# Two-layer decode attention: both wq at the head of the stream, PV in pieces, and another order of the last slabs

## The chip, the core and the metric

The kernel runs on one NeuronCore of a Trainium2 chip. The core has TensorE (PE, matrix products into PSUM), VectorE (DVE), ScalarE (ACT), GpSimd (POOL), and SyncE (SP), whose queue here only issues DMAs. Sixteen DMA engines move data between HBM and the on-chip memory. The metric is the device time of one execution in microseconds; the time of a kernel is the median of its runs.

## The reference

Two independent problems, A and B, have the same shapes. Each decodes one token for a batch of 2, with 32 query heads on 16 key/value heads of width 128, over the last 4096 positions of a cache:

```python
q = (x @ wq).reshape(B, Sq, Hq, Dh).transpose(0, 2, 1, 3)    # x: 2 x 1 x 576, wq: 576 x 4096
...
k = jnp.repeat(k_cache[:, :, Sk - W:, :], rep, axis=1) # W = 4096, rep = 2
v = jnp.repeat(v_cache[:, :, Sk - W:, :], rep, axis=1)
scores = jnp.einsum("bhqd,bhkd->bhqk", q, k) * (Dh ** -0.5)
p = _softmax(scores, axis=-1)
o = jnp.einsum("bhqk,bhkd->bhqd", p, v)
return o.transpose(0, 2, 1, 3).reshape(B, Sq, Hq * Dh) @ wo        # wo: 4096 x 576
```

The two results are concatenated along the last axis. All inputs and outputs are bf16.

## The kernel before

**Slabs.** The heads are worked in 16 steps s, eight for A and eight for B (`ND = 16`). A step takes four (batch, head) pairs: their keys are one slab K of 128 x 16384 bf16 (4096 KB), their values another slab V. Slabs land in `ring`, which has four slots (`NR = 4`).

**The stream.** A list `stream` fixes the order in which SP issues the large loads. The item number n goes into slot n % 4, and its DMA waits for the last reader of item n - 4 (`deps = [reader[n - NR]]`). SP is in order: a DMA that waits holds up every DMA behind it. The list begins Q0 (A's wq), K0, K1, V0, K2, V1, Q1 (B's wq), K3, V2, K4, V3, ..., because Q1 is put in at step `WQ_AT = 3`. wq has 576 rows; 512 go into a ring slot and the last 64 into the small tile `wqr`, by a second DMA. The output weights `wo` are loaded per group of two steps, just ahead of one of the K slabs. The last V slab (V15) is loaded as five pieces (64, 32, 16, 8 and 8 of 128 column blocks), each with its own semaphore.

**One step.** (a) `do_X` (L407): eight DVE transposes bring K to the form that PE needs. (b) `do_S` (L428, L431): PE forms the scores in two PSUM banks. (c) `do_max` (L440) takes maxima per row; `do_nm` turns them on PE (`Tm`, L446), reduces them (L453) and scales them (L458); `do_exp` spreads the result (L463, L470), takes exp on ACT (L475) and transposes the weights p to `pC` (L481). (d) `do_sum` turns the row sums on PE (L487), adds them (L494), takes the reciprocal (L499) and spreads it (L500, L506). (e) `do_PV` (L522): 32 matmuls of p with V into the bank `ACC`, for the step before, s - 1; ACT then evicts `ACC` (L534). (f) For step s - 2, `do_comb` (L555) gathers the evicted sums into `OT`, `do_norm` (L571) normalises on DVE, and once per two steps `do_redist` and `do_proj` (L592, L622) multiply with `wo`. Of the last two steps each is projected by itself. In the last V slab, the final two pieces go through `do_PVb` (L543), which writes `OT` directly.

**The q projection.** `do_qproj(G)` (L359, L367, L373, L381) makes q for two steps: ten matmuls into two of the banks `tb`, two evictions on ACT, one transpose and four copies on DVE. Four groups serve A and run before step 0. The four of B run inside step 3, one after every second transpose of K. The last reader of a wq slot is the last matmul of its fourth group.

**Order.** Each engine runs its operations in the order of the program text, and operations wait for each other by semaphores; nothing is reordered later. On PE, an operation that waits holds up all behind it. The four banks `st` hold two steps' scores; the two banks `tb` are taken in turn by all small jobs.

Of the kernel before, what the change touches and what calls it, by code (L numbers as in the profile page):

```python
# [6 lines left out]
BF16 = mybir.dt.bfloat16  # L7
# [52 lines left out]
def build_kernel(nc, probs, out, cfg=None):  # L60
    cfg = dict(cfg or {})
    NR = cfg.get("NR", 4)
    NKT = cfg.get("NKT", 5)
    NPT = cfg.get("NPT", 3)
    LS = 1
    NZQ = 2
    WQ_AT = cfg.get("WQ_AT", 3)

    x0, k0, v0, wq0, wo0 = probs[0]
    NPROB = len(probs)  # L70
    Bb, _one, D = x0.shape
    _, Hkv, Sk, Dh = k0.shape
    HD = wq0.shape[1]
# [7 lines left out]
    JR = 16  # L81
    NRD = NJ // JR
    SPP = Hkv // 2
    ND = SPP * NPROB
    NG = ND // 2
    GPP = SPP // 2
    NFC = D // 128
    DREM = D - 128 * NFC
    assert DREM * 2 == 128 and NFC * HD == SLABW
    HH = HD // 2  # L90
# [8 lines left out]
    PIECES = [(0, 64), (64, 96), (96, 112), (112, 120), (120, 128)]  # L99
    NPC = len(PIECES)  # L100
# [5 lines left out]
    with es:  # L106
        block = es.enter_context(nc.Block())
        sb = lambda name, shape, dt: es.enter_context(nc.sbuf_tensor(name, shape, dt))
        ring = sb("ring", [128, NR, SLABW], BF16)
        xt = sb("xt", [128, NKT, 1024], FP32)  # L110
        wqr = sb("wqr", [128, HH], BF16)
        wob = sb("wob", [128, 2, 8, NOUT], BF16)
        xT = sb("xT", [128, NPROB, NXC, 128], BF16)
        x_dup = sb("x_dup", [Bb, NPROB, 2, DREM, 2], BF16)
# [40 lines left out]
        wq_sem = [sem("wq%d" % r) for r in range(NPROB)]  # L155
# [42 lines left out]
            return last  # L198
        x_cd = S.add("dve", f_xd, [x_zd, x_dma], "xdup")

        stream = []
        for s_ in range(ND + LS):
            if s_ == 0 or s_ == WQ_AT:
                stream.append(("Q", 0 if s_ == 0 else 1))
            if s_ < ND:
                stream.append(("K", s_))
            if s_ >= LS:
                stream.append(("V", s_ - LS))
        pos = {key: n for n, key in enumerate(stream)}
        w_at = {}  # L210
        for G in range(NG):
            s_ = 2 * G + 2 if by_group(G) else 2 * G + 1
# [3 lines left out]
        pieces = []  # L216
# [3 lines left out]
        qproj = {}  # L220
# [3 lines left out]
        def issue_slab(n):  # L224
            kind, D_ = stream[n]
            if kind == "Q":
# [16 lines left out]
        def issue_wq(n, P):  # L243
            wqP = probs[P][3]
            r = n % NR
            deps = [reader[n - NR]] if n >= NR else []
            slab_dma[n] = dma_op("sp", ring_sem[r], 1, lambda e: e.dma_start(
                ring[:, r, :], wqP[0:NFC * 128, :].rearrange("(p s) n -> p (s n)", s=NFC)).then_inc(ring_sem[r], 16), deps, "wq%d" % P)
            deps = [qproj[(P * GPP - 1, 1)]] if P >= 1 else []
            wq_dma[P] = dma_op("sp", wq_sem[P], 1, lambda e: e.dma_start(  # L250
                wqr[:, :], wqP[NFC * 128:D, :].rearrange("r (h n) -> r h n", h=2)).then_inc(wq_sem[P], 16), deps, "wqr%d" % P)

        def issue_wo(G):
            woP = probs[G // GPP][4]
# [90 lines left out]
        def do_qproj(G):  # L345
            P = G // GPP
            nq = pos[("Q", P)]
            issue_until(nq)
            evs = []
            for nb in range(2):  # L350
                hf = nb
                c0 = nb * HH + 512 * (G % GPP)

                def fn(e, bank, c0=c0, hf=hf):
                    last = None
                    for ch in range(NFC + 1):
                        w_ = ring[:, nq % NR, ch * HD + c0:ch * HD + c0 + 512] if ch < NFC else wqr[:, c0 - hf * HH:c0 - hf * HH + 512]
                        x_ = xT[:, P, ch if ch < NFC else NFC + hf, :]
                        last = e.matmul(bank[:, 0:512], x_, w_, start=(ch == 0), stop=(ch == NFC))  # L359
                    return last  # L360
                n, bank, op = tb_job(fn, "q%d_%d" % (G, nb), [slab_dma[nq], wq_dma[P], op_xev])
                qproj[(G, nb)] = op
                reader[nq] = op
                d = [op]
                if G >= 1:
                    d.append(chain[(G - 1, "qtr")])
                evs.append(S.add("act", lambda e, bank=bank, nb=nb: e.activation(qrow[:, 512 * nb:512 * nb + 512], bank[:, 0:512], ACTF.Copy),  # L367
                                 d, "qrow%d_%d" % (G, nb)))
                tb_consumer[n] = evs[-1]
            d = list(evs)  # L370
            if G >= 1:
                d.append(qkeep[G - 1])
            chain[(G, "qtr")] = S.add("dve", lambda e: e.transpose(qtr[:].bitcast(FP32), qrow[:].bitcast(FP32)), d, "qtr%d" % G)  # L373

            def f_keep(e):
                last = None
                v = qtr[:].rearrange("d (t l r f w p) -> d l w t r f p", t=2, l=2, r=2, f=2, w=32)
                o = qk[:, G, :, :, :].rearrange("d l (f p) (b t r) -> d l b t r f p", f=2, b=Bb, t=2)
                for l_ in range(2):
                    for b in range(Bb):  # L380
                        last = e.tensor_copy(o[:, l_, b], v[:, l_, b])  # L381
                return last
            qkeep[G] = S.add("dve", f_keep, [chain[(G, "qtr")]], "qkeep%d" % G)
# [52 lines left out]
        def do_max(s, jh):  # L436
            d = [Sop[(s, 4 * jh + 3)]]
            if s >= 1:
                d.append(chain[(s - 1, "Tm")])
            chain[(s, "max", jh)] = S.add("dve", lambda e: e.tensor_reduce(  # L440
                m1[:, jh:jh + 1], ST[2 * (s % 2) + jh][:, :], AX.X, ALU.max), d, "max%d_%d" % (s, jh))

        def do_nm(s):
            def fT(e, bank):
                for jh in range(2):
                    last = e.transpose(bank[0:1, 128 * jh:128 * jh + 128], m1[:, jh:jh + 1], ident_f[:])  # L446
                return last
            n, bank, op = tb_job(fT, "Tm%d" % s, [chain[(s, "max", 0)], chain[(s, "max", 1)], p_ident_f])
            chain[(s, "Tm")] = op
            d = [op]  # L450
            if s >= 1:
                d.append(chain[(s - 1, "nMrep")])
            tb_consumer[n] = S.add("dve", lambda e: e.tensor_reduce(  # L453
                nM[0:1, :], bank[0:1, 0:256].rearrange("o (a p) -> o p a", p=8), AX.X, ALU.max, negate=True), d, "nM%d" % s)
            d = [tb_consumer[n]]
            if s >= 1:
                d.append(chain[(s - 1, "bias")])
            chain[(s, "nMrep")] = S.add("dve", lambda e: e.tensor_scalar(  # L458
                nMrep[0:1, :].rearrange("o (a c) -> o a c", c=8),
                nM[0:1, :].unsqueeze(1).broadcast_to([1, 16, 8]), SCALE, None, ALU.mult), d, "nMrep%d" % s)  # L460
# [90 lines left out]
        def do_comb(D_):  # L551
            def f(e):
                last = None
                for j4 in range(4):
                    last = e.matmul(OT[:, 0:8], acc_sb[:, 128 * j4:128 * j4 + 128], ident_r[:, 8 * j4:8 * j4 + 8],  # L555
                                    start=False, stop=True, skip_group_check=True)
                return last
            op = S.add("pe", f, [acc_ev[D_], ot_zero[D_], ot_da[0], init["ident_r"]], "comb%d" % D_)
            comb[D_] = op
            ot_pe[0] = op  # L560
# [81 lines left out]
                out[:, 0, P * NOUT + half * NH:P * NOUT + (half + 1) * NH], out_sb[32 * half:32 * half + Bb, P, :]).then_inc(out_sem, 16),  # L642
                [e_ops[(P, half)]], "out%d_%d" % (P, half))

        for G in range(GPP):
            do_qproj(G)
            if G == 0:
                do_zq(0)
        init_small()

        for s in range(ND):
            D2 = s - 2
            for u in range(NU):
                do_X(s, u)
                if u >= 1:
                    do_S(s, u - 1)
                if u == 1 and s + 1 < ND:
                    do_zq(s + 1)
                if u == 5:
                    do_max(s, 0)  # L660
                if D2 >= 0:
                    if u == 1:
                        do_comb(D2)
                    elif u == 2:
                        do_norm(D2)
                    elif u == 4 and D2 % 2 == 1:
                        do_redist(D2 // 2)
                    elif u == 6 and D2 % 2 == 1:
                        do_proj(D2)
                        if D2 == SPP - 1:  # L670
                            do_E(0, False)
                if s == WQ_AT and u % 2 == 0:
                    do_qproj(GPP + u // 2)
            do_S(s, NU - 1)
            do_max(s, 1)
            do_nm(s)
            do_exp(s)
            if s >= LS:
                do_PV(s - LS, range(NRD), None)
            do_sum(s)  # L680
        D_ = ND - 2
        do_comb(D_)
        do_norm(D_)
        do_proj(D_)
        D_ = ND - 1
        issue_until(len(stream) - 1)
        for n_ in range(NPC - 2):
            do_PV(D_, range(PIECES[n_][0] // JR, PIECES[n_][1] // JR), pieces[n_])
        do_PVb(D_, NPC - 2)
        do_comb(D_)  # L690
        do_PVb(D_, NPC - 1)
# [9 lines left out]
        for e in ENGS:  # L701
            n = 0
# [89 lines left out]
```

## Time and profile before

| | |
|---|---|
| median of 3 runs | 374.55 us (374.13 to 374.67) |
| the profiled execution | 374.36 us, of it a span of 372.6 us from the first to the last instruction |
| read from HBM | 153.10 MB, 411 GB/s over the span |
| DMA queue of SP | 96.2% of 16 engines |
| PE busy / DVE / ACT | 261.4 (70%) / 225.4 (60%) / 64.1 us (17%) |
| granted clock of TensorE, mean | 0.834 |
| `xt<-ring` transposes, L407 | 128, mean 1212 ns |
| PV matmuls, L522 | 508 seen, 40.7 us busy |
| DVE waiting for B's K slabs | 24.0 us in 7 waits |
| a 4096 KB slab of B, issue to landing, median | K 31.0 us, V 34.1 us |

The span is cut into 40 equal slices of 9.3 us in the page's second part. A line of a stretch gives its bounds and length in us, then the busy time and number of instructions for PE, PE's weight loads, DVE, ACT and POOL, then the granted clock of TensorE, the share of DMA busy, and GB/s. Packets are counted whole where they start, so the DMA numbers of very short stretches jump. A line of the timeline gives the start, the time to the end of the last of so many merged instructions, the engine, the line of the code, and in brackets how long the engine was idle before and what ended it. Matmul ends are modelled.

### The profile page before, as it was taken

The numbers are of one execution on the slowest core, as the hardware profiler recorded it, in microseconds if no ns is written. First come the engines' busy times: TensorE is split into PE (matmuls) and PEld (weight loads), VectorE is DVE, ScalarE is ACT, GpSimd is POOL, SyncE is SP. The second block draws the span as 40 slices with busy tenths as digits, with TensorE's granted clock in tenths as the row PEclk, the third lists the DMA queues.
The fourth block names the chain that finished last, engine by engine and source line by source line (L and its number), as shares of the span: only waits on it lengthen the run. The fifth ranks groups of instructions, "written<-read, shape, count | busy, mean of one in ns | idle before, by whom it ended". The sixth has DMA issues, their size and how long they took to land.

```text
span 372.6 us, 3781 instructions
## 1 busy us (share of the span) xinstructions
PE 261.4 (70%) x1533; PEld 100.5 (27%) x1536; DVE 225.4 (60%) x346; ACT 64.1 (17%) x203; POOL 5.2 (1%) x13
## 2 busy tenths in 40 slices
PE   0486687875776988795966857694956768395685
PEld 0132232221322323332422223231322223132232
DVE  0049586935354859595937676684837675573761
ACT  1050112022212111213030210303030211202011
POOL 5000000000000000000000000000000000000000
PEclk9996969987897588989875969788796969677688
DMA  8999999999969999999999999999999999999990
GB/s 338 440 405 450 412 442 443 406 441 440 419 260 420 408 443 434 422 450 421 424 433 422 447 429 427 429 422 441 414 444 429 422 443 421 436 412 441 410 395 24
DMA packets 7865, 153.34 MB, mean 412 GB/s; under 512 B 796, under 2 KB 1832, under 8 KB 2472
## 3 DMA queue, kind: packets, MB, share of 16 engines
q1 hardware_dynamic: 7836, 153.10, 96.2%
q8 instruction: 12, 0.20, 0.2%
q14 instruction: 5, 0.04, 0.0%
q10 hardware_dynamic: 12, 0.01, 0.0%
HBM read 153.10 MB, written 0.00 MB: 411 GB/s over the span
## 4 chain that ended last, share of the span: by engine, by line
DMA 49%; PE 30%; DVE 16%; ACT 2%; issue 2%; SPq 0%; DVEq 0%
DMA ring<-in_B_k_cache_dram 39%; PE st L431 17%; DVE xt L407 10%; DMA ring<-in_A_k_cache_dram 6%; PE tb L359 4%; PE acc L522 4%; DMA wqr<-in_A_wq_dram 4%; DVE m L440 2%; PE st L428 2%; PE ot L622 1%; ACT qrow L367 1%; DVE qtr L373 1%; DVE pC L481 1%; PE tb L463 1%; DVE nM L453 1%
## 5 line engine op out<-in xcount | busy, mean ns | idle before, releaser
L407 DVE STREAM_TRANSPOSE xt<-ring 128x1024 f32<-128x1024 f32 x128 | 149.3, 1212 | 31.1 <-DMA ring<-in_B_k_cache_dram 24.0
L431 PE MATMUL st<-xt,zq 128*128 128x512 bf16 x512 | 153.5, 450 | 8.9 <-DVE xt L407 8.5
L431 PEld LDWEIGHTS st<-xt,zq 128*128 128x128 bf16 x512 | 49.6, 108 | 93.8 <-issue 44.2
L428 PE MATMUL st<-mcol,mrow 4*128 4x512 bf16 x32 | 14.7, 460 | 44.9 <-DVE xt L407 44.8
L522 PE MATMUL acc<-ring,pC 128*32 128x512 bf16 x508 | 40.7, 474 | 0.0
L440 DVE TENSOR_REDUCE m<-st 128x1 f32<-128x512 f32 x32 | 21.9, 685 | 27.9 <-PE st L431 27.9
L481 DVE STREAM_TRANSPOSE pC<-pR 128x512 bf16<-128x512 bf16 x32 | 22.1, 711 | 24.0 <-ACT pR L475 24.0
L470 ACT ACTIVATE bias_sb<-tb 128x1 f32<-128x1 f32 x16 | 2.7, 171 | 174.9 <-PE tb L463 174.9
L359 PE MATMUL tb<-ring,xT 128*128 128x512 bf16 x61 | 19.4, 441 | 6.2 <-DMA wqr<-in_A_wq_dram 5.2
L475 ACT ACTIVATE pR<-st,bias_sb 128x512 bf16<-128x512 f32 x32 | 21.7, 682 | 0.5
L373 DVE STREAM_TRANSPOSE qtr<-qrow 128x512 f32<-128x512 f32 x8 | 5.7, 706 | 26.1 <-ACT qrow L367 26.1
L522 PEld LDWEIGHTS acc<-ring,pC 128*32 128x32 bf16 x508 | 14.7, 111 | 15.7 <-issue 9.2
L428 PEld LDWEIGHTS st<-mcol,mrow 4*128 4x128 bf16 x32 | 3.0, 94 | 51.6 <-DVE xt L407 48.0
L500 PE MATMUL tb<-rs,ones_f 1*128 1x8 f32 x32 | 6.8, 282 | 12.8 <-DVE rs L499 12.8
L446 PE MATMUL tb<-ident_f,m 128*1 128x128 f32 x32 | 6.1, 271 | 12.5 <-DVE m L440 12.5
L463 PE MATMUL tb<-ones_f,nMrep 1*128 1x1 f32 x32 | 6.4, 265 | 12.0 <-DVE nMrep L458 12.0
L395 ACT ACTIVATE zq<-qk 32x32 bf16<-32x32 bf16 x64 | 14.2, 222 | 1.8 <-DVE qk L381 1.2
L367 ACT ACTIVATE qrow<-tb 128x512 bf16<-128x512 f32 x16 | 9.4, 597 | 29.6 <-PE tb L359 28.6
L534 ACT ACTIVATE acc_sb<-acc 128x512 bf16<-128x512 f32 x16 | 9.6, 597 | 15.7 <-PE acc L522 15.7
L494 DVE TENSOR_REDUCE ssum<-tb 1x8 f32<-1x256 f32 x16 | 6.2, 388 | 9.3 <-PE tb L487 9.3
L453 DVE TENSOR_REDUCE nM<-tb 1x8 f32<-1x256 f32 x16 | 6.6, 412 | 7.5 <-PE tb L446 7.5
L359 PEld LDWEIGHTS tb<-ring,xT 128*128 128x128 bf16 x64 | 6.7, 110 | 15.7 <-issue 9.9
(56 smaller groups left out, 97.3 us busy)
## 6 DMA issues: line engine op xcount, KB each, us to landing
ring<-in_A_k_cache_dram SPq DMA_DIRECT2D x8, 4096.0 KB, 24.4
ring<-in_A_v_cache_dram SPq DMA_DIRECT2D x8, 4096.0 KB, 25.8
ring<-in_B_k_cache_dram SPq DMA_DIRECT2D x8, 4096.0 KB, 31.0
ring<-in_B_v_cache_dram SPq DMA_DIRECT2D x7, 4096.0 KB, 34.1
wob<-in_A_wo_dram SPq DMA_DIRECT2D x4, 1152.0 KB, 27.8
ring<-in_A_wq_dram SPq DMA_DIRECT2D x1, 4096.0 KB, 12.3
ring<-in_B_wq_dram SPq DMA_DIRECT2D x1, 4096.0 KB, 18.4
wob<-in_B_wo_dram SPq DMA_DIRECT2D x3, 1152.0 KB, 36.1
```

Source lines behind the costliest of these rows:

```text
L359: last = e.matmul(bank[:, 0:512], x_, w_, start=(ch == 0), stop=(ch == NFC))
L367: evs.append(S.add("act", lambda e, bank=bank, nb=nb: e.activation(qrow[:, 512 * nb:512 * nb + 512], bank[:, 0:512], ACTF.Copy), d, "qrow% ...
L395: last = e.activation(zq[pr_, :, s % NZQ, 24 + 32 * a:32 + 32 * a], qk[pr_, G, s % 2, :, :], ACTF.Copy)
L407: Xop[(s, u)] = S.add("dve", lambda e: e.transpose(xt[:, i % NKT, :].rearrange("k (j w) -> k j w", w=64), ring[:, n % NR, jh * 8192:jh * 8 ...
L428: last = e.matmul(bank[:, 0:512], mrow[:, :], mcol[:, :], start=True, stop=False)
L431: last = e.matmul(bank[:, 0:512], zq[:, p4, s % NZQ, w0:w0 + 128], mv, start=False, stop=jq == 3 and p4 == 3)
L440: chain[(s, "max", jh)] = S.add("dve", lambda e: e.tensor_reduce(m1[:, jh:jh + 1], ST[2 * (s % 2) + jh][:, :], AX.X, ALU.max), d, "max%d_% ...
L453: tb_consumer[n] = S.add("dve", lambda e: e.tensor_reduce(nM[0:1, :], bank[0:1, 0:256].rearrange("o (a p) -> o p a", p=8), AX.X, ALU.max, ...
L463: n, bank, op = tb_job(lambda e, bank: e.matmul(bank[:, 0:1], nMrep[0:1, 0:128], ones_f[0:1, 0:1], start=True, stop=True), "bias%d" % s, [ ...
L475: chain[(s, "exp", jh)] = S.add("act", lambda e, jh=jh: e.activation(pR[:, jh, :], ST[2 * (s % 2) + jh][:, :], ACTF.Exp, bias=bias_sb[:, 0 ...
L481: chain[(s, "pC", jh)] = S.add("dve", lambda e, jh=jh: e.transpose(pC[:, s % NPT, 64 * jh:64 * jh + 64, :].rearrange("k j c -> k (j c)"), ...
L522: last = e.matmul(ACC[32 * cb:32 * cb + 32, 0:512], pC[:, D_ % NPT, j0_:j0_ + 4, :].rearrange("k j c -> k (j c)"), ring[:, n % NR, j0_ * 1 ...
```

## The change

B's wq goes to the head of the stream, right behind A's, and all eight groups of the q projection run before step 0. `wqr` gets a part for each problem, so B's remainder no longer waits for A's last projection. The PV of the step before is split in three: two of its eight rounds (four matmuls each) stand before `do_nm`, two between `do_nm` and `do_exp`, four after `do_exp`. At the end, the sum of the last step and the gathering, normalisation and projection of step 14 are placed between the pieces of the last PV.

```diff
@@
-    WQ_AT = cfg.get("WQ_AT", 3)
@@
-        wqr = sb("wqr", [128, HH], BF16)
+        wqr = sb("wqr", [128, NPROB, HH], BF16)
@@
-        stream = []
+        stream = [("Q", P) for P in range(NPROB)]
         for s_ in range(ND + LS):
-            if s_ == 0 or s_ == WQ_AT:
-                stream.append(("Q", 0 if s_ == 0 else 1))
             if s_ < ND:
                 stream.append(("K", s_))
             if s_ >= LS:
@@ issue_wq
-            deps = [qproj[(P * GPP - 1, 1)]] if P >= 1 else []
             wq_dma[P] = dma_op("sp", wq_sem[P], 1, lambda e: e.dma_start(
-                wqr[:, :], wqP[NFC * 128:D, :].rearrange("r (h n) -> r h n", h=2)).then_inc(wq_sem[P], 16), deps, "wqr%d" % P)
+                wqr[:, P, :], wqP[NFC * 128:D, :].rearrange("r (h n) -> r h n", h=2)).then_inc(wq_sem[P], 16), [], "wqr%d" % P)
@@
-        for G in range(GPP):
+        for G in range(NG):
             do_qproj(G)
             if G == 0:
                 do_zq(0)
@@
-                if s == WQ_AT and u % 2 == 0:
-                    do_qproj(GPP + u // 2)
             do_S(s, NU - 1)
             do_max(s, 1)
+            if s >= LS:
+                do_PV(s - LS, range(0, 2), None)
             do_nm(s)
+            if s >= LS:
+                do_PV(s - LS, range(2, 4), None)
             do_exp(s)
             if s >= LS:
-                do_PV(s - LS, range(NRD), None)
-            do_sum(s)
-        D_ = ND - 2
-        do_comb(D_)
-        do_norm(D_)
-        do_proj(D_)
+                do_PV(s - LS, range(4, NRD), None)
+            if s < ND - 1:
+                do_sum(s)
         D_ = ND - 1
         issue_until(len(stream) - 1)
-        for n_ in range(NPC - 2):
-            do_PV(D_, range(PIECES[n_][0] // JR, PIECES[n_][1] // JR), pieces[n_])
+        do_PV(D_, range(PIECES[0][0] // JR, PIECES[0][1] // JR), pieces[0])
+        do_sum(D_)
+        do_comb(D_ - 1)
+        do_norm(D_ - 1)
+        do_PV(D_, range(PIECES[1][0] // JR, PIECES[1][1] // JR), pieces[1])
+        do_proj(D_ - 1)
+        do_PV(D_, range(PIECES[2][0] // JR, PIECES[2][1] // JR), pieces[2])
         do_PVb(D_, NPC - 2)
         do_comb(D_)
         do_PVb(D_, NPC - 1)
```

More of the change, by code (lines that the diff above doesn't have):

```diff
@@ L356, in fn @@
                     for ch in range(NFC + 1):
-                        w_ = ring[:, nq % NR, ch * HD + c0:ch * HD + c0 + 512] if ch < NFC else wqr[:, c0 - hf * HH:c0 - hf * HH + 512]
+                        w_ = ring[:, nq % NR, ch * HD + c0:ch * HD + c0 + 512] if ch < NFC else wqr[:, P, c0 - hf * HH:c0 - hf * HH + 512]
                         x_ = xT[:, P, ch if ch < NFC else NFC + hf, :]
```

## The prediction

> **What bounds the kernel now.** I read the page's slices first, then the busy time by stretches of some 31 us.
>
> ```profile
> DMA  8999999999969999999999999999999999999990
> GB/s 338 440 405 450 412 442 443 406 441 440 419 260 420 408 443 434 422 450 421 424 433 422 447 429 427 429 422 441 414 444 429 422 443 421 436 412 441 410 395 24
> 61.00:92.00 31.00, 21.64 (x136) 8.07 (x138) 19.45 (x31) 7.55 (x24) 0.00 (x0) 0.88 1.02 436
> 92.00:124.00 32.00, 23.13 (x125) 8.84 (x125) 16.04 (x35) 6.94 (x18) 0.00 (x0) 0.82 0.87 370
> 124.00:155.00 31.00, 26.43 (x142) 10.05 (x140) 22.03 (x31) 3.36 (x12) 0.00 (x0) 0.81 1.00 429
> ```
>
> The DMA engines are full nearly everywhere and no compute engine is, so the stream of 153.1 MB sets the time. Its rate from 30 to 342 us is 426 to 436 GB/s in every such stretch but one (mean 430, last column). Only two places lose time: the stretch from 92 to 124 us (370 GB/s, slice 12 of the page), and the last slice, where the stream has ended and the rest of the arithmetic runs. Next, 1 us stretches and the timeline around the dip.
>
> ```profile
> 108.00:109.00 1.00, 1.00 (x6) 0.46 (x5) 0.00 (x0) 0.00 (x0) 0.00 (x0) 1.00 0.15 66
> 109.00:110.00 1.00, 1.00 (x6) 0.42 (x5) 0.00 (x0) 0.60 (x1) 0.00 (x0) 1.00 0.00 0
> 110.00:111.00 1.00, 1.00 (x5) 0.29 (x3) 0.16 (x1) 0.60 (x1) 0.00 (x0) 1.00 0.00 0
> 109.79 0.38 PE L359 MATMUL tb<-wqr,xT 128*128 128x512 bf16 x1
> 110.20 0.54 SPq L240 DMA_DIRECT2D ring<-in_A_v_cache_dram  x1
> ```
>
> The queue is empty. SP issues V3 at 110.20, right after the last of B's q projections (L359, 109.79 + 0.38): V3 goes into the slot that B's wq held, and everything on SP stands behind it. Quarter-microsecond stretches show no packet from 108.25 to 111.50, 3.25 us. By bytes it is more: 32 us x (1 - 370/430) = 4.5 us, the uneven end and the restart included.
>
> Last the end, from the timeline.
>
> ```profile
> 346.47 3.50 DVE L407 STREAM_TRANSPOSE xt<-ring 128x1024 f32<-128x1024 f32 x3 [4.39 <-DMA ring<-in_B_k_cache_dram]
> 358.65 0.69 DVE L440 TENSOR_REDUCE m<-st 128x1 f32<-128x512 f32 x1 [1.57 <-PE st L431]
> 359.40 0.38 PE L446 MATMUL tb<-ident_f,m 128*1 128x128 f32 x2 [0.78 <-DVE m L440]
> 360.84 3.18 PE L522 MATMUL acc<-ring,pC 128*32 128x512 bf16 x32
> 361.96 1.38 DVE L481 STREAM_TRANSPOSE pC<-pR 128x512 bf16<-128x512 bf16 x2 [1.48 <-ACT pR L475]
> 363.95 0.58 PE L487 MATMUL tb<-ident_f,rsum 128*1 128x128 f32 x2
> 365.26 0.39 PE L500 MATMUL tb<-rs,ones_f 1*128 1x8 f32 x2 [0.73 <-DVE rs L499]
> 368.46 0.60 ACT L534 ACTIVATE acc_sb<-acc 128x512 bf16<-128x512 f32 x1 [2.60 <-PE acc L522]
> ```
>
> K15 lands at 346.4, and from there the compute chain, not V15, decides. V15's five pieces are issued at 334.3 to 336.8 and take 26.8 to 29.3 us: they land at 361.1, 363.6, 364.8, 365.4 and 366.1. The weights pC for PV15 are there at 363.34 (361.96 + 1.38), but PE still does PV14, the sum of slab 15 and the projection of slab 14, and starts PV15 near 366.4.
>
> **Part 1: wq of B moves to the head.** Its two DMAs (4.194 + 0.524 MB) go ahead of K0, K1, V0, wo0, K2 and V1 on SP; no byte is added, and with two halves in wqr the second remainder waits for nothing. What has to be shown is that the queue now runs dry nowhere else. The stream in its new order: the first 30 us move 402 GB/s x 30 = 12.06 MB, and 430 GB/s follows. The two wq and their remainders are 9.44 MB and end near 23.9; 1.2 us lie between last byte and landing for A's wq (4.72 MB moved by 13.2 in the 4 us stretches, first use 14.49), so B's lands near 25.1. K0 ends at 33.7, K1 43.5, V0 53.3, wo0 and K2 65.8, V1 75.6, K3 85.4, V2 95.2, wo1 and K4 108.
>
> Each issue must come 1.3 us before its forerunner ends (110.20 to 111.50). The compute: A's four groups still end at 26.9, after B's wq has landed. The transposes of q (L373) begin at 19.59, 22.89, 25.42 and 27.58, so a group takes 2.66 us (2.16 to 3.30), and four more take 10.7 (8.6 to 13.2). The first slab's transposes, before at 30.39, begin at 41.1 (39.0 to 43.6). A slab takes 17.1 us (the next starts at 47.52) and frees its K slot after 10.8 (V1 issued at 41.21).
>
> - V0 waits for A's last projection, 26.94; needed by 42.2.
> - K2 waits for B's last projection, near 37.6; needed by 52.0.
> - V1 waits for slab 0's K: 41.1 + 10.8 = 51.9; needed by 64.5.
> - K3 waits for slab 1's K: 41.1 + 17.1 + 10.8 = 69.0 (66.9 to 71.5); needed by 74.3.
> - V2 waits for PV0, 16 us into slab 1 (63.53 - 47.52): 74.2; needed by 84.1.
> - K4 waits for slab 2's K, 86.1, needed by 93.9; V3 for PV1, 91.3, needed by 106.7.
>
> The smallest cover is K3's, 5.3 us (2.8 at the slow end); once it is gone, each further microsecond costs one. Slab 3 no longer holds the other four groups (it ran from 87.66 to 121.46, 33.8 us against 17.1), so compute reaches slab 4 near 109.5 instead of 121.46 and waits for K from there on, as now. A pair of slabs and half a wo are 8.98 MB, 20.9 us of stream against 17.1 of compute, so no new bound arises. **Gain between 3.25 and 4.5 us; I take 3.9, the middle,** since the edges of the hole are partly real loss and partly packets counted late.
>
> **Part 2: PV of the slab ahead in pieces.** No matmul is added: 32 become 8 + 8 + 16. In the middle of the stream this is worth nothing, since steps wait for K. The added wait: the first 8 stand before the maximum's transposes (L446) and need V of slab s-1; behind them on PE are L446, L463, and by them the whole softmax. V14 is issued at 329.42 and takes 26.7, so it is there at 356.1; PE comes to it at 358.6. Cover 2.5 us, price nothing.
>
> In the last slab 32 matmuls took 3.1 us at clock 0.50 (97 ns each), and 1.84 us (57.5 ns) at 1.00 in slab 1. Eight (0.46 to 0.78) lie under the maximum (358.65 to 359.34), eight under nM and nMrep (359.82 to 360.47), sixteen (0.92 to 1.55) end by 362.5 under exp and pC. PV15 may thus start at 363.4.
>
> **Part 3: order of the end.** From 363.4, all warm: 16 matmuls of piece 0, 0.92; sum to reciprocal to L500, 1.11 (341.02 to 342.13); to L555, 0.32 (365.26 to 365.58); comb 0.10; 8 matmuls of piece 1, 0.46, which cover slab 14's normalisation; its projection, 8 of the 16 that take 1.07, 0.53; 4 matmuls of piece 2, 0.23; 0.09 to the eviction. That is 3.76, eviction at 367.15 against 368.46: 1.3 saved. With piece 0 cold (1.55) and the sum cold (1.31) it is 367.98: 0.5 saved. All cold, twice the matmul time there and some 0.6 more after the eviction, it is 1.1 lost. The pieces land before they are needed in each. **I take 0.9, between the first two:** clock 1.00 is the row from 364.7 on, 0.50 the one just before.
>
> The clock is told by its row: it fell to 0.50 from 361.3 to 364.7 although PE had worked some 1.3 of the 2.8 us before (half-microsecond stretches).
>
> [...]
>
> **Sum.** The profiled execution took 374.36 us (span 372.6, 1.76 around it; 0.19 below the median of 374.55). 374.36 - 3.9 - 0.9 = 369.6.
>
> **Rivals.**
> - *Hole closed, end gives back.* PE stalls between L487 and L500 with the clock at half. For it: that clock at 361 to 365, and PE idling from 362.5 to 363.4 in the new order. Against: 1.00 after 364.7. 374.36 - 3.9 + 1.1 = 371.6.
> - *The hole only moves.* The change doesn't do what it says: K3 is late at the head. For it: compute starts 11 us later. Against: the cover of 5.3. With a hole as long as the old one, 374.36 - 0.9 = 373.5.
> - *Slower: V14 holds up the softmax.* Place: the 8 matmuls ahead of L446 in slab 15. If V14 lands after 358.6, the end waits one for one; it decides from 2.5 us of lateness, and outweighs the gain of 4.8 from 7.3. For it: V follows K on one queue, 9.8 us behind. Against: 356.1 above. At 10 us late, 374.36 - 4.8 + 7.5 = 377.1.
>
> **Chances.** Forecast 0.72, end gives back 0.14, hole moves 0.07, slower 0.07. The range is from 374.36 - 4.5 - 1.3 = 368.6 less 0.3 (spread of the runs) = 368.3, to 374.36 - 3.25 + 1.1 = 372.2; it takes in the first rival and leaves out 0.14. 0.2% is 0.75 us, about what can be told from no change. Forecast and first rival are faster, 0.86, and so is part of the second: 0.89; same 0.04; slower 0.07.
>
> **What would show it.** No slice below 390 GB/s between the first and the last two; slab 0's transposes near 41 and K3 issued near 69; the last K near 342.5; the eviction of PV15 (L530 in the new file) 21.1 us after it instead of 22.0. A slice with a dip before 90 us makes the forecast wrong, and so does a wait of L442 for V.

## The result and the profile after

The changed kernel takes 370.81 us (median of 5 runs, 369.73 to 371.95) against 374.55 us (5 runs): ratio 0.9899, 95% interval 0.9864 to 0.9935. A second set on another chip, shown below, gave 371.66 us and a ratio of 0.9921 (0.9890 to 0.9952). The profiled execution took 369.99 us, its span 368.2 instead of 372.6. The change leaves the order of the last slabs in the stream as it was; only the work behind them is in another order.

The slices of the page and the stretches of the stream, to be laid beside those of before (columns as there):

```profile
DMA  8999999999999999999999999999999999999990
GB/s 342 413 441 434 416 419 450 441 409 452 417 436 420 445 407 453 417 444 420 434 425 438 424 428 435 434 424 436 427 437 417 438 420 448 413 416 436 422 394 37
61.00:92.00 31.00, 26.22 (x147) 9.24 (x145) 22.54 (x32) 5.18 (x17) 0.00 (x0) 0.83 1.02 437
92.00:124.00 32.00, 27.77 (x170) 10.43 (x173) 24.33 (x33) 4.50 (x19) 0.00 (x0) 0.85 1.00 429
```

The slice with 260 GB/s is gone, and the stretch from 92 to 124 us moves 429 GB/s instead of 370. No other slice has dipped in its place. The head, from SP's timeline, shows the issues of K2, V1, K3 and V2:

```profile
35.91 0.54 SPq L237 DMA_DIRECT2D ring<-in_A_k_cache_dram  x1
50.69 0.53 SPq L237 DMA_DIRECT2D ring<-in_A_v_cache_dram  x1
68.07 0.54 SPq L237 DMA_DIRECT2D ring<-in_A_k_cache_dram  x1
72.45 0.53 SPq L237 DMA_DIRECT2D ring<-in_A_v_cache_dram  x1
```

They were forecast at 37.6, 51.9, 69.0 and 74.2. Behind each of them the stream goes on: no slice of the page from 25 to 95 us is below 409 GB/s. The end, from the timeline:

```profile
342.30 3.50 DVE L403 STREAM_TRANSPOSE xt<-ring 128x1024 f32<-128x1024 f32 x3 [5.02 <-DMA ring<-in_B_k_cache_dram]
354.74 0.69 DVE L436 TENSOR_REDUCE m<-st 128x1 f32<-128x512 f32 x1 [1.83 <-PE st L427]
356.93 1.05 PE L518 MATMUL acc<-ring,pC 128*32 128x512 bf16 x16
358.05 1.38 DVE L477 STREAM_TRANSPOSE pC<-pR 128x512 bf16<-128x512 bf16 x2 [1.48 <-ACT pR L471]
359.53 1.05 PE L518 MATMUL acc<-ring,pC 128*32 128x512 bf16 x16 [1.56 <-DVE pC L477]
363.52 0.60 ACT L530 ACTIVATE acc_sb<-acc 128x512 bf16<-128x512 f32 x1 [1.30 <-PE ot L618]
364.88 1.12 PE L618 MATMUL ot<-wob,oTn 128*2 128x288 bf16 x8 [0.26 <-DVE oTn L567]
```

K15 lands at 342.3 instead of 346.47, 4.17 us earlier: nearly the whole gain of 4.4 us in the span. Counted by bytes (the GB/s of 4 us stretches, summed), the stream's first 140 MB have moved at 328.0 us instead of 332.1, 4.1 us earlier. PV14's last 16 matmuls end under exp, and PV15 starts as soon as pC is there, as meant. Yet from K15 to the end it is 25.9 us against 26.13. The eviction comes 0.8 us sooner after K15, but then the last projection takes 1.12 us where it took 0.66 before.

### The profile page after: what moved, and what is told of

Its sections match the earlier page's. It is cut to its first block, busy times and chain, and to the rows that moved or that the text cites. A ratio compares the mean times of both kernels' runs of the same rounds, so it can differ in the third digit from the quotient of the medians.

```text
span 368.2 us, 3787 instructions
## 1 busy us (share of the span) xinstructions
PE 259.6 (71%) x1535; PEld 96.7 (26%) x1536; DVE 226.0 (61%) x346; ACT 62.5 (17%) x203; POOL 5.2 (1%) x13
## 4 chain that ended last, share of the span: by engine, by line
DMA 58%; PE 26%; DVE 12%; ACT 2%; issue 1%; SPq 0%
DMA ring<-in_B_k_cache_dram 40%; PE st L427 17%; DMA ring<-in_A_k_cache_dram 15%; DVE xt L403 7%; PE tb L355 5%; DMA wqr<-in_A_wq_dram 4%; PE st L424 2%; DVE m L436 2%; DVE pC L477 1%; PE ot L618 1%; ACT pR L471 1%; ACT qrow L363 0%; PE acc L518 0%; DVE qtr L369 0%; DVE nM L449 0%
## 5 line engine op out<-in xcount | busy, mean ns | idle before, releaser
L427 PE MATMUL st<-xt,zq 128*128 128x512 bf16 x512 | 157.0, 461 | 1.9 <-DVE xt L403 1.5
L427 PEld LDWEIGHTS st<-xt,zq 128*128 128x128 bf16 x512 | 50.9, 110 | 89.3 <-issue 50.7
L424 PE MATMUL st<-mcol,mrow 4*128 4x512 bf16 x32 | 15.6, 487 | 52.8 <-DVE xt L403 52.8
L518 PE MATMUL acc<-ring,pC 128*32 128x512 bf16 x508 | 36.5, 383 | 1.6 <-DVE pC L477 1.6
L355 PE MATMUL tb<-ring,xT 128*128 128x512 bf16 x63 | 18.6, 420 | 6.5 <-DMA wqr<-in_A_wq_dram 5.6
L483 PE MATMUL tb<-ident_f,rsum 128*1 128x128 f32 x32 | 6.3, 278 | 12.4 <-ACT pR L471 12.4
L518 PEld LDWEIGHTS acc<-ring,pC 128*32 128x32 bf16 x508 | 9.3, 95 | 15.5 <-issue 11.8
L596 ACT ACTIVATE Rsb<-tb 128x16 bf16<-128x16 f32 x7 | 1.3, 185 | 59.5 <-PE tb L588 59.5
L496 PEld LDWEIGHTS tb<-rs,ones_f 1*128 1x128 f32 x32 | 5.8, 223 | 18.8 <-DVE rs L495 18.8
```

The costliest lines, as they stand in the source:

```text
L424: last = e.matmul(bank[:, 0:512], mrow[:, :], mcol[:, :], start=True, stop=False)
L427: last = e.matmul(bank[:, 0:512], zq[:, p4, s % NZQ, w0:w0 + 128], mv, start=False, stop=jq == 3 and p4 == 3)
L496: n2, bank2, op = tb_job(lambda e, bank: e.matmul(bank[:, 0:8], ones_f[0:1, 0:128], rs[0:1, 0:8], start=True, stop=True), "rsbm%d" % s, [c ...
L518: last = e.matmul(ACC[32 * cb:32 * cb + 32, 0:512], pC[:, D_ % NPT, j0_:j0_ + 4, :].rearrange("k j c -> k (j c)"), ring[:, n % NR, j0_ * 1 ...
```

## The experiments

### One part alone, and the same slot freed otherwise

**The head alone.** Of the diff only the stream, `wqr` and the eight groups at the head; PV in one piece and the old end.

```diff
@@ the changed kernel
-                do_PV(s - LS, range(0, 2), None)
...
-                do_PV(s - LS, range(2, 4), None)
...
-                do_PV(s - LS, range(4, NRD), None)
-            if s < ND - 1:
-                do_sum(s)
+                do_PV(s - LS, range(NRD), None)
+            do_sum(s)
...
```

> The stream and the q projections as in the changed kernel, PV in one piece and the end in the old order. Theory (the emptied queue was nearly all of the gain): no stretch without packets, last K slab lands near 342.3 us as in the changed kernel, span 368.2 + 0.2 = 368.4, about 370.2 us. Rival (the new order of PV and of the end brings half or more of the gain): 372 us or more.

Measured: 370.38 us, ratio 0.9884 (0.9853 to 0.9916), span 368.4, K15 at 342.55, 25.85 us from there to the end. The head alone brings all of the gain.

**PV and the end alone.** The old stream with Q1 at step 3, the new PV and end.

```diff
@@ the changed kernel
-        stream = [("Q", P) for P in range(NPROB)]
+        stream = []
         for s_ in range(ND + LS):
+            if s_ == 0 or s_ == WQ_AT:
+                stream.append(("Q", 0 if s_ == 0 else 1))
...
-        for G in range(NG):
+        for G in range(GPP):
             do_qproj(G)
...
+                if s == WQ_AT and u % 2 == 0:
+                    do_qproj(GPP + u // 2)
```

> PV in pieces and the new end, on the old stream with B's wq at step 3. Theory: the 3.25 us without packets near 108 us stay, last K slab near 346.4; from the last K slab to the end 25.9 instead of 26.1 us, span 372.4, about 374.2 us. If the clock stays up through the last projection, as it did before, the end is 0.5 shorter still: 373.7. Rival (PV and the end bring half or more): 372.3 or less.

Measured: 374.41 us, ratio 0.9984 (0.9961 to 1.0008), span 372.5. The hole is there, 2.75 us without packets (108.25 to 111.00) against 3.25; the stretch and two of its microseconds:

```profile
92.00:124.00 32.00, 23.08 (x136) 8.88 (x136) 18.08 (x39) 6.85 (x18) 0.00 (x0) 0.93 0.87 370
109.00:110.00 1.00, 1.00 (x7) 0.45 (x5) 0.00 (x0) 0.52 (x2) 0.00 (x0) 1.00 0.00 0
110.00:111.00 1.00, 0.75 (x4) 0.13 (x2) 0.45 (x1) 0.51 (x1) 0.00 (x0) 1.00 0.00 0
```

Two numbers missed. K15 landed at 345.15, 1.3 us sooner than in the old kernel. V3 is issued 0.3 us sooner (109.91 us), and by bytes the stream is 0.3 us ahead (140 MB at 331.9 us). The other 1.0 us is in the landing of this one slab, for the K slab before it lands at 322.72 here and at 322.76 there; why is open. A single landing thus tells the stream's progress only to about 1 us. And from K15 to the end it took 27.35 us instead of 25.9: this half of the change, on its own, shows no gain.

**Head and PV in pieces, old end.** `do_sum` for every step, then step 14's gathering, normalisation and projection, then the three pieces of PV15.

```diff
@@ the changed kernel
-            if s < ND - 1:
-                do_sum(s)
+            do_sum(s)
+        do_comb(ND - 2)
+        do_norm(ND - 2)
+        do_proj(ND - 2)
...
-        do_sum(D_)
-        do_comb(D_ - 1)
-        do_norm(D_ - 1)
...
-        do_proj(D_ - 1)
```

> The head of the changed kernel and PV in pieces, but the sum of slab 15 and slab 14's normalisation and projection before the last PV as in the old end. Theory: PV14 is done when pC is, so the sum starts 0.5 us earlier than in the old kernel against the last K slab; from the last K slab to the eviction of the last PV 21.5 us, between the 22.0 of the old and the 21.2 of the changed kernel; span near 368.2. Rival (only the order of the end matters): 22.0.

Measured: 370.62 us, ratio 0.9888 (0.9862 to 0.9915), span 368.8. From K15 to the eviction of PV15 it took 22.34 us, more than either kernel, so neither theory foresaw it. Its timeline and a row of the clock, with the same two lines of the head alone, show why: 24 merged matmuls of PV15 and the stretch from 362 to 363 us, first here, then there.

```profile
361.66 2.88 PE L518 MATMUL acc<-ring,pC 128*32 128x512 bf16 x24
362.00:363.00 1.00, 1.00 (x14) 0.60 (x10) 0.00 (x0) 0.00 (x0) 0.00 (x0) 0.50 0.00 0
```

```profile
362.44 1.68 PE L518 MATMUL acc<-ring,pC 128*32 128x512 bf16 x24
362.00:363.00 1.00, 1.00 (x24) 0.84 (x28) 0.00 (x0) 0.00 (x0) 0.00 (x0) 1.00 0.00 0
```

The same matmuls in the same order take 2.88 us at clock 0.50 or 1.68 us at 1.00. The clock, not the order, made this end long.

**The old place, but the slot freed early.** The old kernel, B's wq at step 3 as before, its four groups in one block ahead of that step.

```diff
@@ the old kernel
             D2 = s - 2
+            if s == WQ_AT:
+                for G in range(GPP, NG):
+                    do_qproj(G)
             for u in range(NU):
...
-                if s == WQ_AT and u % 2 == 0:
-                    do_qproj(GPP + u // 2)
```

> The old kernel with B's wq where it was in the stream, but its four groups in one block before step 3 instead of one after every second transpose inside it. Theory (the queue ran empty because the slot of B's wq was held until the fourth group, not because of wq's place): the groups end near 92 us, V3 is issued then instead of at 110.2, the hole is gone, and the time is that of the head alone, about 370.4 us. Rival (wq's place at the head is what matters, for instance by the rate of the stream): the hole moves or stays, 373.5 to 374.5.

Measured: 370.13 us, ratio 0.9875 (0.9847 to 0.9903), span 368.4, K15 at 342.34. V3 and K5 on SP's timeline, and the stretch:

```profile
90.26 0.54 SPq L240 DMA_DIRECT2D ring<-in_A_v_cache_dram  x1
102.42 0.54 SPq L240 DMA_DIRECT2D ring<-in_A_k_cache_dram  x1
```

```profile
92.00:124.00 32.00, 25.13 (x152) 9.61 (x156) 24.53 (x35) 3.59 (x14) 0.00 (x0) 0.89 1.00 430
```

V3 is issued at 90.26 instead of 110.20 and the stretch moves 430 GB/s. So what cost the time was the slot held through step 3 by projections spread between the transposes; that wq leads the stream is one way of freeing it, not a cause by itself.

### The cover at the head

DVE is given memsets of the whole transpose buffer `xt` ahead of slab 0, which holds up every later slab. One, then three:

```diff
+        def do_delay():
+            d = qkeep[NG - 1]
+            for _ in range(3):
+                d = S.add("dve", lambda e: e.memset(xt[:].rearrange("k n w -> k (n w)"), 0.0), [d], "delay")
+            init["delay"] = d
```

> The changed kernel with one memset of the whole transpose buffer (20 KB a partition, about 4.8 us by the rate of the OT memset, 512 elements in 0.48) on DVE ahead of slab 0. Theory (the head has cover): K3 is issued near 72.9 instead of 68.07 and the queue still holds V1, which lands at 78.2; no stretch without packets, about 370.5 us, no change. Rival (the head has no cover left, the prediction's was luck): up to 4.8 us more, 375.

> The same with three memsets, about 14.4 us. Theory: K3 is issued near 82.5, 1.3 us before its first packet, while V1's last packets go near 76.5: a hole of about 7 us after V1 and nothing later, about 377.5 us. Rival (compute catches up and hides it, or a later wait is hit as well): 371, or 385.

Measured: with one memset (4.33 us) 371.66 us, ratio 0.9917 (0.9884 to 0.9949); with three 381.38, ratio 1.0179 (1.0150 to 1.0209). SP's issue of K3 and the first transpose of step 15 with the one:

```profile
72.62 0.54 SPq L237 DMA_DIRECT2D ring<-in_A_k_cache_dram  x1
...
342.21 3.50 DVE L411 STREAM_TRANSPOSE xt<-ring 128x1024 f32<-128x1024 f32 x3 [5.75 <-DMA ring<-in_B_k_cache_dram]
```

With the three, the same two lines and three stretches of the stream:

```profile
83.00 0.54 SPq L237 DMA_DIRECT2D ring<-in_A_k_cache_dram  x1
...
351.48 3.50 DVE L411 STREAM_TRANSPOSE xt<-ring 128x1024 f32<-128x1024 f32 x3 [5.69 <-DMA ring<-in_B_k_cache_dram]
64.00:68.00 4.00, 3.17 (x15) 1.06 (x14) 2.71 (x3) 0.00 (x0) 0.00 (x0) 1.00 0.64 229
76.00:80.00 4.00, 4.00 (x13) 1.34 (x11) 3.11 (x3) 0.00 (x0) 0.00 (x0) 0.66 0.31 131
80.00:84.00 4.00, 3.97 (x18) 1.36 (x18) 2.97 (x3) 0.00 (x0) 0.00 (x0) 1.00 0.00 0
```

K3 comes 4.55 us later in the first and K15 lands at 342.21, as without the memset: all of it is covered. In the second K3 is issued at 83.00, 14.9 us later, and K15 lands at 351.48, 9.2 us later. 14.9 - 9.2 = 5.7 us were covered. The time is 3.9 us above the 377.5 foreseen: I had counted on 7 us of hole after V1, but the stretches show two holes, since V1 itself (issued at 66.05) came too late as well, and both runs have a longer end, 27.8 and 27.9 us from K15 on, which is the next subject.

### The clock in the end

The steps of the end, read from the timelines of eight profiled executions whose last step waits for K15, in us ("changed, again" is the second set's; "old place, one block" is the old place with the slot freed early):

| kernel | K15 lands | to the maximum | to pC | to the eviction of PV15 | to the output's eviction | to the end | sum |
|---|---|---|---|---|---|---|---|
| before | 346.47 | 12.18 | 4.69 | 5.12 | 2.06 | 2.08 | 26.13 |
| changed | 342.30 | 12.44 | 4.69 | 4.09 | 2.53 | 2.15 | 25.90 |
| changed, again | 341.99 | 13.26 | 4.68 | 5.19 | 2.56 | 2.12 | 27.81 |
| head alone | 342.55 | 13.17 | 4.69 | 3.77 | 2.07 | 2.15 | 25.85 |
| PV and end alone | 345.15 | 12.57 | 4.69 | 5.39 | 2.56 | 2.14 | 27.35 |
| head, PV in pieces | 342.26 | 12.26 | 4.68 | 5.40 | 2.06 | 2.14 | 26.54 |
| old place, one block | 342.34 | 13.42 | 4.69 | 3.77 | 2.07 | 2.11 | 26.06 |
| one memset | 342.21 | 13.02 | 4.69 | 5.37 | 2.56 | 2.15 | 27.79 |

The step to the eviction of PV15 takes one of two lengths, whatever the order, 3.8 to 4.1 or 5.1 to 5.4, and so does the step behind it, 2.06 or some 2.55. Where a step is short, the clock's row reads 1.00 there (1.00 from 361 to 364 us in the head alone, 3.77 us); where long, 0.50 in part (0.50 from 361 to 364 us in the head with PV in pieces, 5.40 us). Two runs test this.

**Idle matmuls in the waits of the new end.** Six ahead of PV15, two between the sum and its reciprocal, two before the last gathering, 128x512, into a bank that nobody reads. (One `do_warm(n)` is `n` times `e.matmul(ST[0][:, 0:512], ident_b[:, :], xt[:, 0, 0:256].bitcast(BF16), start=True, stop=True)`.)

```diff
@@ the changed kernel
+        do_warm(6)
         do_PV(D_, range(PIECES[0][0] // JR, PIECES[0][1] // JR), pieces[0])
-        do_sum(D_)
+        do_sum(D_, 2)
...
         do_PVb(D_, NPC - 2)
+        do_warm(2)
         do_comb(D_)
```

> The changed kernel with ten idle matmuls of 128x512 in PE's waits of the end (six before the last PV, two between the sum and its reciprocal, two before the last gathering), written to a bank that nobody reads. Theory (the clock falls in the end because PE has too little work in the window before): clock 1.00 through the last projection, which takes 0.66 instead of 1.12; 25.4 us from the last K slab to the end instead of 25.9, span near 367.8. Rival (the clock falls by its own time, or the extra matmuls delay the chain): 25.9 or more.

Measured: 369.93 us, ratio 0.9872 (0.9842 to 0.9902), span 368.9. Its last projection and 12 of step 15's first scores:

```profile
346.00 4.64 PE L427 MATMUL st<-xt,zq 128*128 128x512 bf16 x12
366.10 0.65 PE L628 MATMUL ot<-wob,oTn 128*2 128x288 bf16 x8 [0.26 <-DVE oTn L577]
```

The clock's row reads 1.00 from 354 to 368 us and the projection takes 0.65 us: that half of the theory holds (from the maximum to the end 12.95 us against 13.46). The four profiles of the new end in the table (changed, changed again, PV and end alone, one memset) show 0.50 there. The sum from K15 missed, 26.57 instead of 25.4, for the scores at the start of step 15 ran slow for longer: the same 12 matmuls, before which nothing was changed, had taken 3.47 us in the changed kernel.

**Idle matmuls also ahead of step 15, old order of PV and end.** The head alone, 16 matmuls where PE waits for K15 and nine in its later waits (the expectation says ten).

```diff
@@ the head alone
+                    if s == ND - 1 and u == 1:
+                        do_warm(16, s - 1)
                     do_S(s, u - 1)
...
+            if s == ND - 1:
+                do_warm(3, s - 1)
             do_nm(s)
+            if s == ND - 1:
+                do_warm(2, s - 1)
             do_exp(s)
...
-            do_sum(s)
+            do_sum(s, 2 if s == ND - 1 else 0)
...
```

> The head of the changed kernel, the old PV and the old end, and idle matmuls into an unread bank: 16 ahead of the scores of step 15, where PE waits for K15, and 10 in its waits after that. Theory (from the last K slab to the end 25.9 to 27.9 us differ by the clock alone): scores 12.0 us instead of 12.2 to 13.4, 3.8 from pC to the eviction, 2.06 on: 24.7 from K15 to the end, span 367.0, about 368.8 us and a smaller spread of the runs. Rival (the clock is not what differs, or the extra matmuls stand in the way): 370 or more.

Measured: 368.97 us, ratio 0.9865 (0.9837 to 0.9892), span 367.2; 12.30, 4.69, 3.77, 2.06 and 2.17 us for the steps of the table, 24.99 in all. It is shorter than every row above, though the same end had a full clock without idle matmuls in two of its profiles (the head alone and the block, 1.00 from 358 to 368 us). The spread of the runs, 368.10 to 370.45, did not shrink as I had expected; the clock still fell at the start of step 15 in the profile (1.00 from 342 to 344 us, then a mean of 0.56 to 346 and of 0.59 to 348 us).

### Another end

**K15 ahead of V13.** Against the changed kernel:

```diff
+        i_k = stream.index(("K", ND - 1))
+        stream[i_k - 1], stream[i_k] = stream[i_k], stream[i_k - 1]
         pos = {key: n for n, key in enumerate(stream)}
...
+                if end and u == 6:
+                    do_PV(D2, range(NRD), None)
```

> The changed kernel with K15 ahead of V13 in the stream, PV13 inside step 15, and PV14 after exp of step 15. Theory (after the change the end is set by the chain from the last K slab, 25.9 us, not by the last V bytes, which land about 19.6 us after that slab): K15 lands near 332.5, the chain waits for V15's pieces, and the end comes about 4 us after the last piece lands near 362: span near 366, about 368 us. Rival (the end is set by the stream and what follows it): 370 or more.

Measured: 371.92 us, ratio 0.9922 (0.9894 to 0.9950), span 370.2: a miss. pC was there at 356.09, 3.3 us earlier than in the changed kernel, but PV15 was evicted only at 366.06. I had put step 13's normalisation behind pC on DVE, and PV14 behind step 13's projection on PE, where it began only near 359.8; V14 lands near 352.5 in this stream, as the last version below shows.

**The same stream, the order mended.** Step 13 is gathered and normalised right behind the last scores, PV14 runs under exp, the projection of step 13 stands between the sum of slab 15 and the spreading of its reciprocal. In all other steps PV is in one piece again, behind exp.

```diff
@@ K15 ahead of V13
             if end:
                 do_comb(D2)
+                do_norm(D2)
             do_nm(s)
             do_exp(s)
...
+            if end:
+                do_PV(s - LS, range(NRD), None)
+                do_redist(D2 // 2)
...
+        do_PV(D_, range(PIECES[0][0] // JR, PIECES[0][1] // JR), pieces[0])
+        do_sum(D_, lambda: do_proj(D_ - 2))
+        do_comb(D_ - 1)
+        do_norm(D_ - 1)
...
```

> K15 ahead of V13 again, with step 15's PE order mended: gathering and normalisation of step 13 right behind the last scores, PV14 behind the bias (under exp), the projection of steps 12 and 13 between the sum of step 15 and its reciprocal, the last PV first after pC. Theory (what stood behind pC in the first try, 9.97 us to the eviction, kept it from the end that the stream allows): the eviction comes within 1.5 us of piece 2 (near 361), end 4.5 us later plus the output's 2.1: span 366.5 to 367.5, about 369 us. Rival (the clock at half and PE's own work set the end): 370 or more.

Measured: 369.08 us, ratio 0.9851 (0.9823 to 0.9878), span 367.5; runs from 367.17 to 370.00. PV15 starts at 357.22, released by V15's first piece and no more by pC (355.79). The eviction is at 363.29, 0.8 us later than foreseen: the clock was at 0.50 from some 354.3 to 361.1 us, and PV15's first 16 matmuls took 1.90 us. Two of the six runs, 367.17 and 367.25 us, had the highest mean clock of the six, 0.841.

**Both together.** The last stream and order, with idle matmuls of 128x256 in PE's waits of steps 14 and 15.

```diff
@@ the order mended
+            if s >= ND - 2:
+                do_warm(5, s)
             do_nm(s)
+            if s >= ND - 2:
+                do_warm(5, s)
             do_exp(s)
+            if s == ND - 2:
+                do_warm(14, s)
...
                 do_redist(D2 // 2)
+                do_warm(10, s)
...
         do_PVb(D_, NPC - 2)
+        do_warm(3, D_)
         do_comb(D_)
```

> K15 ahead of V13 as in the second try, and idle matmuls of 128x256 in PE's waits of the last two steps. Theory (the two gains are of different parts: the swap takes the chain from K15 off the end, the clock shortens what is left after V15's pieces): clock 1.00 from 334 us on, the eviction of the last PV near 361.3, span 365.5, about 367.3 us. Rival (both shorten the same stretch): 367.2 in span, 369 us.

> The changed kernel itself once more, beside the fastest version on one chip. Theory: the last K slab near 342.3 as in every kernel with the slot of B's wq freed early; from there 25.9 to 27.9 us by the clock; 369.7 to 372 us in its runs. Rival (the spread comes from the stream): the last K slab differs by more than 0.5 us from 342.3.

Measured on one chip: 367.11 us, ratio 0.9802 (0.9772 to 0.9831), span 365.9, against 371.66 us, ratio 0.9921 (0.9890 to 0.9952), for the changed kernel. Its runs lie between 366.82 and 367.59, those of the changed kernel between 370.64 and 372.06. K15 of the changed kernel landed at 341.99, within 0.5 us of 342.3, so its spread is in the end and not in the stream. PV14, PV15's first piece and the last projection on the timeline:

```profile
352.50 1.91 PE L533 MATMUL acc<-ring,pC 128*32 128x512 bf16 x32 [0.46 <-DMA ring<-in_B_v_cache_dram]
357.41 1.05 PE L533 MATMUL acc<-ring,pC 128*32 128x512 bf16 x16 [1.61 <-DMA ring<-in_B_v_cache_dram]
363.04 0.66 PE L633 MATMUL ot<-wob,oTn 128*2 128x288 bf16 x8 [0.26 <-DVE oTn L582]
```

PE now waits for the V pieces themselves. This is the fastest version of the study; what is left after the stream is the eviction at 361.67, the last gathering, one projection and the output.

## Why the prediction was right, and where it was not

**The hole.** Right in place, cause and size. I had taken 3.9 us between 3.25 (empty time) and 4.5 (bytes); the stream is 4.1 us ahead by bytes in the changed kernel and 4.1 to 4.2 in the head alone and the block, and the medians of the latter two are 4.1 and 4.35 us below the old kernel's of the same set. That the slot, not wq's place, decides is shown by the block.

**The cover at the head.** 5.3 us at K3 were forecast, about 5.7 us measured. The rival "the hole only moves" was real and has its price, but its point lies beyond what the kernel does: with K3 4.55 us later the last K slab still landed at the same time.

**PV in pieces, and the end.** Here the term "I take 0.9" was mis-sized. In the profiled execution the eviction of PV15 came 21.2 us after K15, where 21.1 was forecast and the old kernel had 22.0; but that is luck of the clock, which in this execution fell only after the eviction (364.5 us against 363.52). In the second one the clock fell ahead of it (362.4 us against 365.12), and it came after 23.1 us. The like-for-like size is the difference of ends at the same clock: 4.09 us from pC to the eviction in the new order at full clock (the changed kernel and the one with idle matmuls) against 3.77 in the old (the head alone, the block, and the old end with idle matmuls). It is a loss of 0.3 us in the profiles, not a gain; the runs of one kernel spread too much to tell 0.3 us. The wrong step is the one that set "32 matmuls took 3.1 us at clock 0.50" of the old end against a new end with warm rates: at full clock PV14 takes 1.91 us in one piece, ends before pC in the old order too, and the sum of slab 15 runs under pC. The new order puts it behind PV15's first piece.

**The rivals.** "End gives back" (371.6) is nearest to the second set's median, 371.66, and named the right place, the clock; the profiled execution, 369.99, is nearest to the forecast. Against the first set's median the forecast was 1.2 us low: the 0.9 of the end did not come, and some executions had the longer end. "V14 holds up the softmax" did not show: in the new order PE begins PV14 at 354.64 right behind the scores; V14, issued at 326.52 and 25.5 us on its way, had landed at 352.0.

**What I weighed of the clock.** The prediction priced the end by the clock's row of one execution. In the two profiled executions of the changed kernel the last fall is at 364.5 and at 362.4 us, and the same instructions took 25.90 and 27.81 us. In the clock records of the kernel before and of the first execution of the changed kernel, each of the 41 and 33 times from one change to the next is a whole number of 3.41 us (3.41 to 23.89 us). The two last falls of the changed kernel are 2.1 us apart, with K15 landing at 342.30 and 341.99: the changes met other instructions in each execution.

No long pause of PE stands ahead of the fall at 364.5: PE's longest pause in the 12 us before was 1.6 us (357.98 to 359.53), and PE was busy for 2.45 us of the last 3.41. In the kernel before, the fall at 361.3 came behind 1.88 us of work in 3.41. With PE's waits filled, the clock read 1.00 from 354 to 368 us in the new end and from 330 to 362 us in the fastest version. That PE's share of work keeps the clock up is my reading of these rows, with modelled matmul ends; no run varied that share alone, and how much work it takes was not shown.

## What to carry to other kernels

When a stream of large transfers is the bound, look for the one stretch in which its queue is empty, and for the reader that holds the next slot: freeing the slot early brought the empty time back in both places tried here (K15 at 342.55 and 342.34 us instead of 346.47), as long as the cover of the places that it delays is not used up (5.7 us at K3). Work that cannot start before a late landing should be priced at both clocks of TensorE before its order is changed, since one profile shows one of them: 24 matmuls of PV15 took 1.68 us at 1.00 in one profile here and 2.88 us at 0.50 in another. At the end of this stream, moving the slab with the long chain ahead of one with a short chain gained nothing at first (371.92 us), and 1.7 to 2.6 us against the changed kernel's two sets once the work behind it was put in the order in which its data lands (369.08).

## What the runs showed of the hardware

The end of one kernel varied by 2 us between executions (25.9 and 27.8 us from K15), which is about the spread of its runs (369.73 to 371.95). The granted clock read 0.50 or 1.00, and its last fall was at 364.5 us in the one execution and at 362.4 us in the other. With PE's waits filled in the last two steps, in the fastest version, the runs stayed within 0.8 us and the clock read 1.00 from 330 to 362 us; the same order without the filling ran from 367.17 to 370.00, on another chip. How much work of PE keeps the clock up was not shown.
